# One core of Trainium2, attention and a gated MLP: the product and cast of a late pair's x^T moved to place 17, the first Strassen weights converted sooner

## The chip, the cores and the metric

The kernel runs on one core of a Trainium2 chip. The metric is the device time of one execution in microseconds (us); smaller is better. The engines are named as the profile names them: PE is TensorE (PEld its weight loads), DVE is VectorE, ACT is ScalarE, POOL is GpSimd and SP is SyncE, which issues most of the transfers. Each engine works off its own queue in order and meets the others through semaphores.

## What is computed

The reference, cut to its core (q and k are drawn about 5.7 times larger than its own setup draws them, the gate's weights 8 times; the three weight matrices arrive as float64):

```python
def _attn_ref(q, k, v):                      # q, k, v: 8 batches, 8 heads, 576 rows, 64 columns
    scores = (1.0 / np.sqrt(D)) * np.matmul(q, k.transpose(0, 1, 3, 2))
    scores = np.where(block_i >= block_j, scores, -1e9)      # blocks of 64 rows, causal
    scores = scores - np.max(scores, axis=-1, keepdims=True)
    attn = np.exp(scores)
    attn = attn / (np.sum(attn, axis=-1, keepdims=True) + 1e-09)
    return np.matmul(attn, v)

def _moe_ref(x, w_gate, w_val, w_out):       # x: 4608 x 512, d_ff = 1536
    gate = 1.0 / (1.0 + np.exp(-(x @ w_gate)))
    return (gate * (x @ w_val) @ w_out)
```

x is the attention's output with the heads side by side: 4608 tokens of 512 columns.

## The kernel before

**Attention, pair by pair.** The 64 heads are worked off as 32 pairs (two heads of a batch side by side on 128 partitions), `p` from 0 to 31; four pairs make a batch. Pairs 0 to 7 run in an early form. The late pairs, from 8 on, are what the change is about. For one of them, `prep` transposes keys and queries on VectorE (L436, into `KQ`) and splits them into a high and a low part: KH and QH by ScalarE (L476, L477), KL and QL by VectorE (L480, L481); GpSimd scales the first queries (L478) and copies the last ones into blocks (L486). `attend` then makes the scores (L397, into three double banks of PSUM), their maxima on VectorE (L536, L627), the exponentials on ScalarE (L551, L633), the 32x32 transposes of the exponentials on VectorE (L729 and on, into `ZV`), and the products with the values on TensorE in two halves (`z_run`). `z_out` copies these products from PSUM to `xT` on ScalarE (L778). The reciprocals of the sums go through memory (L639) and come back broadcast to all rows as `rb` (L647).

**finish.** `finish` ends a pair: GpSimd multiplies `xT` by `rb` (one product L806, two small ones L811), ScalarE casts the result to the high part `XH` (L813), GpSimd makes the low part `XL` (L828), and a store of `xT` is queued (L820). For the last pair VectorE does the products. `XH` and `XL` are the MLP's input.

**The MLP in between.** As soon as a batch's four pairs are done, its MLP with the first third of d_ff starts (`mlp1`): 144 matmuls of 128x512 a batch, 96 for gate and value (L163) and 48 for the output (L170). They are strewn between the attention's matmuls, so that TensorE has work while the other engines make the exponentials. Their results go to two banks named `m`. A gate is read by ScalarE (L202), a value by VectorE (L210); the product is split by ScalarE (L216, `hH`) and GpSimd (L217, `hL`); an output bank is evicted by ScalarE (L955) and stored (L958).

**What sets the order.** The order of a late pair is written out as a table, `REST`: a step's name and its number of places, 36 in all; at every place about one matmul of the MLP is dealt out. The steps are: AV (second half of the products of the pair before, and `z_out`), s and t (scores), sl (scores of the two smallest blocks), tr3, trt, tr2 (transposes), ml (maxima and exponentials of the two smallest blocks), r (reciprocals), trl, half (first half of this pair's products), k and q (both halves of `prep` for the next pair), and FX (`finish` for the pair before). Pair 8 has a table of its own (`JOIN`). In the late pairs an engine's instructions are chained in the order in which they are emitted (`line`); the gates, splits and low parts of the MLP are chained too, but the eviction L955 isn't: the scheduler places it. `LOADS` says at which place SyncE issues which transfer: v0, v1 (values), rb (the broadcast), xs (the store of `xT`), k0 to q3 (keys and queries), rr (the reciprocals to memory).

`KEEP` sets how many matmuls of the running MLP are kept back when a batch ends, to cover the time until the next batch's input is there; its second number counts from pair 8 on. Ahead of the products, `fill` adds a few tiny matmuls, so many that the count of TensorE's instructions fits a window.

**Behind the last pair** stand the last two MLPs (288 matmuls, what was kept back, and the last batch's tail), and under them the conversion of the first weights for the other two thirds of d_ff, which run as Strassen products (from L1340 on). `fetch_gv` loads float64 weights, `sums_gv` turns them into float32 and makes the sums, `split_gv` splits them; `x_sums` and `x_split` do the same for the tokens. The two first conversions are `early[0]` and `early[1]`; `early[0]` is fetched at the start of the last pair.

Of the kernel before, what the change touches and what calls it, by code (L numbers as in the profile page):

```python
# [20 lines left out]
N2 = 512  # L21
NX = 256
AHEAD = 3
KEEP = (52, 48)
WINDOW, MOST, FRONT = (140, 152), 24, 53

CONV_DUE = ([(0, 5), (0, 10), (1, 10), (2, 10), *((p, 9) for p in range(3, 7))], [(6, 1), (7, 2), (7, 8), (8, 1)])
# [2 lines left out]
         ("tr3", 1), ("r", 0), ("ld", 0))  # L30
ALONE = (("S3", 1), ("TR2", 1), ("warm", 0), ("k", 1), ("S2", 1), ("q", 1), ("m3", 0), ("m2", 0), ("TRt", 1), ("t", 1), ("TRl", 1), ("sl", 1), ("AV", 2),
         ("tr3", 1), ("r", 0), ("FX", 0), ("ld", 0))
REST = (("AV", 0), ("s", 0), ("t", 9), ("sl", 3), ("tr3", 2), ("trt", 3), ("tr2", 0), ("ml", 0), ("r", 0), ("trl", 0),
        ("half", 6), ("k", 4), ("q", 3), ("FX", 6))
JOIN = (("s", 0), ("t", 9), ("AV", 8), ("sl", 3), ("tr3", 2), ("trt", 3), ("tr2", 0), ("ml", 0), ("trl", 0), ("half", 2),
        ("r", 2), ("k", 2), ("q", 5))
TURN = (("s3", 1), ("TR2", 1), ("k", 0), ("s2", 1), ("TRt", 1), ("q", 0), ("t", 1), ("TRl", 1), ("sl", 1), ("AV", 1),
        ("tr3", 1), ("r", 0), ("tr2", 1), ("trl", 1), ("trt", 3))
N_FIRST = 7
LOADS = {0: "v0", 5: "rb", 8: "xs", 10: "k0", 12: "k1", 14: "k2", 16: "k3", 18: "v1", 23: "rr", 25: "q0", 27: "q1", 29: "q2", 32: "q3"}  # L40
JOIN_LOADS = {0: "k0", 3: "k1", 6: "k2", 9: "k3", 11: "v0", 16: "v1", 21: "q0", 24: "q1", 27: "q2", 30: "q3", 33: "rr"}
NV = 21
TICKS = 12
# [9 lines left out]
def attn_glu_kernel(ctx: ExitStack, tc: tile.TileContext, q, k, v, w_gate, w_val, w_out, out):  # L53
# [26 lines left out]
    def behind(ins, other):  # L80

        tc.add_manual_dep(ins, other.name, mybir.DependencyInfo(mybir.DependencyClass.NoSync,
                                                                mybir.DependencyReason.DATA), reason="order")
# [143 lines left out]
    with ExitStack() as s2:  # L227
# [105 lines left out]
        def load_in_turn(p, what, now):  # L333

            kind, i = what[0], what[1]
            dmas = ()
            if what == "rr":
                now(what)
            elif what in ("rb", "xs"):
                if waiting[what]:  # L340
                    waiting[what].pop()()
            elif kind == "v" and p + 1 < len(pairs):
                dmas = values_load(p + 1, int(i))
            elif kind in "kq" and p + 2 < len(pairs):
                dmas = (rows_load(p + 2, kind, int(i), nc.sync),)
            for dma in dmas:
                tc.add_manual_dep(dma.ins, dealt[0].name, mybir.DependencyInfo(mybir.DependencyClass.Sync,
                                                                               mybir.DependencyReason.DATA), reason="pace")
                line("q", dma)
                if kind == "v":  # L350
                    loads["SP"] = dma.ins
# [3 lines left out]
        last, loads, q_copied, recent = {}, {}, [], []  # L355
# [722 lines left out]
        def fetch_gv(g, q, gv, j, held=False, half=None):  # L1078
            raw, T = cv_tiles() if half is None else half_tiles()
            c = slice(None) if half is None else slice(half * P // 2, (half + 1) * P // 2)  # L1080
            src = (w_gate, w_val)[gv].rearrange("(kh c p) (a fh q n) -> kh c a q p fh n", kh=2, c=KC, fh=2, q=2, n=P)
            rawv = raw.rearrange("p (kh fh n) w -> p kh fh (n w)", kh=2, fh=2)
            fetch([rawv[:, kh] for kh in range(2)], [src[kh, j, F1 // 4 + g, q][:, :, c] for kh in range(2)], held)
            return raw, T

        def sums_gv(raw, T, held=False, **kw):

            Tn = T.rearrange("p s n -> p (s n)")
            m = 4 * T.shape[-1]
            to_f32(raw, Tn[:, :m], Tn[:, m:], held, **kw)  # L1090
            nc.vector.tensor_sub(out=T[:, 4], in0=T[:, 0], in1=T[:, 1])
            nc.vector.tensor_add(out=T[:, 1], in0=T[:, 1], in1=T[:, 3])
            nc.vector.tensor_sub(out=T[:, 5], in0=T[:, 3], in1=T[:, 4])
            return nc.vector.tensor_sub(out=T[:, 6], in0=T[:, 2], in1=T[:, 5]).ins
# [28 lines left out]
        def x_load(k, j, c0):  # L1123

            t0, nk = blocks[k]
            XB = cv.tile([P, 4, NX], F32, name="XB", bufs=2)
            v = XB[:, 0:4].rearrange("p (kh th) n -> p kh th n", kh=2)
            src = xT_d.rearrange("b (kh c p) s -> c b p kh s", kh=2, c=KC)[j]
            for th in range(2):
                a = 0  # L1130
                while a < NX:
                    b, o = divmod(t0 + th * nk + c0 + a, S)
                    m = min(S - o, NX - a)
                    d = nc.sync.dma_start(out=v[:, :, th, a:a + m], in_=src[b][:, :, o:o + m])
                    if "SP" in last2:
                        behind(d.ins, last2["SP"])
                    mark2("SP", d)
                    a += m
            return XB

        def x_sums(XB, eng, other=None):
            t1 = eng.tensor_sub(out=XB[:, 1], in0=XB[:, 1], in1=XB[:, 0])  # L1142
            if other:
                behind(t1.ins, other)
            return t1.ins
# [95 lines left out]
        early, early_x = [], []  # L1241

        def early_work(p, tick):

            if p == NP and tick == 0:
                n_conv[1] += 1
                next(conv_o)
            when = p - (n - 1), tick
            if when in ((0, 0), (1, 0)):
                early.append(fetch_gv(0, 0, 0, len(early)))  # L1250
                early_x.append(x_load(0, len(early_x), 0))
        for p in range(n + 1):
            early_work(p, 0)
            pr = prep(p + 1) if p + 1 < n else iter(())
            now = attend(p) if p < n else None
            tick = 0
            steps = (ALONE if p < NP else FIRST if p < N_FIRST else TURN if p == N_FIRST else
                     JOIN if p == N_FIRST + 1 else REST)
            ticks = sum(places for _, places in steps)
            lined[0] = line if N_FIRST < p < n else no_line  # L1260
            for what, places in steps:
# [23 lines left out]
                if p <= N_FIRST and new and p:  # L1285
                    rate = (left - KEEP[0]) / (4 * TICKS)
                elif p > N_FIRST and (new or what == steps[0][0]):
                    i = p % NP
                    rate = max(0, left - KEEP[1]) / (ticks - tick + (NP - 1 - i) * PLACES) if i or new else 1.0
                for _ in range(places if now else 6 if what == "AV" else 0):  # L1290
                    pe_ticks.append(pe_last[0])
                    acc += rate
                    while acc >= 1:
# [4 lines left out]
                        if ins is not None:  # L1298
# [7 lines left out]
                            if len(pe_ticks) > ahead_by:  # L1306
                                behind(ins, pe_ticks[-1 - ahead_by])
                    if now and p > N_FIRST and tick in (JOIN_LOADS if p == N_FIRST + 1 else LOADS):
                        load_in_turn(p, (JOIN_LOADS if p == N_FIRST + 1 else LOADS)[tick], now if p + 1 < n else lambda x: None)
                    tick += 1  # L1310
# [4 lines left out]
                load(p + 2, "v")  # L1315
            prev = now

        sums_gv(*early[0], alone=last["DVE"])
        x_sums(early_x[0], nc.vector, last["DVE"])
        sums_gv(*early[1], alone=last["DVE"])  # L1320
        s_at.close()
# [136 lines left out]
        early = [fetch_gv(0, 0, 1, j) for j in range(KC)]  # L1458
# [128 lines left out]
```

## Time and profile before

| | us |
|---|---|
| three runs, median | 1255.37 (1252.44 to 1256.64) |
| profiled execution | 1257.75 |
| its span, first to last instruction | 1256.0 |
| early pairs and first late pair, 0 to 149.71 | 149.71 |
| late pairs 9 to 31, 149.71 to 624.56 | 474.85 |
| MLP behind the last pair, 624.56 to 709.68 | 85.12 |
| Strassen products, 709.68 to 1256.0 | 546.32 |

TensorE is busy for 93% of the span, VectorE for 70%, ScalarE for 46%, GpSimd for 27%. These shares mix stages of different kinds, so the sections below go by stretch. The boundaries are the starts of the scores of a pair on TensorE (149.71 is pair 9, 215.00 pair 12) and the end of the last product with the values.

### The profile page before, as it was taken

Reading aid. Unit: us, or ns where it says so; the run is one execution under the profiler, and the core shown is the slowest. Engines: PE = TensorE matmul, PEld = TensorE weight load, DVE = VectorE, ACT = ScalarE, POOL = GpSimd, SP = SyncE. Lnnn points to the kernel's source line nnn. Section 1 sums busy time; section 2 is a strip of 40 time slices with the busy share of each in tenths; the row PEclk is TensorE's granted clock in tenths of the full one; section 3 lists DMA queues with packets and bytes.
Section 4 is the critical chain, followed back from the end, with each engine's and each line's share of the span. In section 5 each row is a group of like instructions: output and inputs, shape, how many; then the busy total and the mean of one; then the engine's idle time right before and its main releaser. Section 6 shows DMA issues by size and latency. Waiting matters only on the chain.

```text
span 1256.0 us, 31932 instructions
## 1 busy us (share of the span) xinstructions
PE 1162.5 (93%) x12843; PEld 927.7 (74%) x12843; DVE 878.0 (70%) x1751; ACT 573.3 (46%) x1372; POOL 345.0 (27%) x424
## 2 busy tenths in 40 slices
PE   8898978788897988879998999999999999999998
PEld 5565767566675767657776888888888888888888
DVE  5876845466464765656498795988999976758564
ACT  5876644445453554545424344354444432333222
POOL 3344424232323242332301111111111235151402
PEclk9998989899898998989999999999999999999999
DMA  7756454465655656546354214275377956253532
GB/s 175 181 133 156 120 124 116 123 161 136 149 141 126 174 118 171 139 112 161 113 156 133 69 51 134 55 201 148 72 217 256 313 178 203 84 184 108 161 105 81
DMA packets 345844, 180.29 MB, mean 144 GB/s; under 512 B 199072, under 2 KB 315616, under 8 KB 345056
## 3 DMA queue, kind: packets, MB, share of 16 engines
q1 hardware_dynamic: 342960, 175.20, 51.2%
q8 instruction: 101, 1.65, 0.6%
q10 hardware_dynamic: 2352, 2.00, 0.5%
q0 software_dynamic: 384, 1.05, 0.2%
q14 instruction: 47, 0.39, 0.1%
HBM read 130.58 MB, written 47.62 MB: 142 GB/s over the span
## 4 chain that ended last, share of the span: by engine, by line
PE 67%; DVE 10%; DMA 8%; POOL 6%; ACT 5%; issue 3%; SPq 1%; DVEq 0%; POOLq 0%; ACTq 0%
PE b L1340 27%; PE bank L397 9%; PE m L1425 8%; PE b L1425 8%; PE m L163 7%; PE m L170 6%; DMA rqk<-in_k_dram 3%; POOL xT L806 2%; ACT P L551 2%; DVE ZV L729 2%; DVE KQ L436 2%; PE bank L163 1%; DMA VR<-in_v_dram 1%; DVE nm L536 1%; DMA XB<-xT_d 1%
## 5 line engine op out<-in xcount | busy, mean ns | idle before, releaser
L1340 PE MATMUL b<-XH,w 128*128 128x512 f32 (+1 forms) x1120 | 320.6, 368 | 0.8 <-ACT p L1358 0.4
L1340 PEld LDWEIGHTS b<-XH,w 128*128 128x128 f32 x1120 | 203.5, 188 | 37.2 <-ACT p L1358 0.8
L1340 PE MATMUL b<-XL,w 128*128 128x512 f32 (+1 forms) x560 | 205.6, 368 | 0.0
L551 ACT ACTIVATE P<-bank,nm 128x512 f32<-128x512 f32 (+3 forms) x256 | 131.8, 524 | 41.4 <-DVE nm L536 41.1
L170 PE MATMUL m<-wo,hH 128*128 128x512 f32 x256 | 99.1, 447 | 36.1 <-ACT raws L955 31.9
L536 DVE TENSOR_REDUCE nm<-bank 128x2 f32<-128x1024 f32 (+3 forms) x128 | 100.9, 812 | 27.4 <-ACT bank L584 25.9
L1340 PEld LDWEIGHTS b<-XL,w 128*128 128x128 f32 x560 | 105.6, 189 | 17.5
L1157 ACT CAST XH<-XB 128x1024 fp32r<-128x1024 f32 (+1 forms) x72 | 66.9, 943 | 87.0 <-DVE XB L1155 49.6
L1425 PE MATMUL m<-wo,hH 128*128 128x512 f32 x288 | 93.2, 389 | 0.0
L163 PE MATMUL m<-XH,wg 128*128 128x512 f32 x240 | 86.9, 416 | 6.9 <-ACT raws L955 6.9
L170 PEld LDWEIGHTS m<-wo,hH 128*128 128x128 f32 x256 | 53.9, 213 | 53.0 <-ACT raws L955 34.1
L1425 PE MATMUL b<-wo,hH 128*128 128x512 f32 x288 | 92.9, 389 | 0.0
L1142 POOL TENSOR_TENSOR XB<-XB 128x256 f32<-128x256 f32 x30 | 24.6, 819 | 246.0 <-DMA XB<-xT_d 169.8
L729 DVE STREAM_TRANSPOSE ZV<-P 128x512 f32<-128x512 f32 (+1 forms) x192 | 84.8, 484 | 6.5 <-ACT P L551 6.5
L163 PE MATMUL m<-XH,wv 128*128 128x512 f32 x240 | 88.5, 424 | 0.0
L1160 DVE TENSOR_TENSOR XL<-XB,XH 128x1024 fp32r<-128x1024 f32 (+1 forms) x72 | 78.6, 1095 | 10.9 <-ACT XH L1157 10.7
L478 POOL TENSOR_SCALAR KQ<-KQ 128x128 f32<-128x128 f32 x24 | 22.4, 934 | 204.0 <-DVE KQ L436 204.0
L588 DVE MEMSET bank<- 64x128 f32 x24 | 4.0, 165 | 106.1 <-PE bank L397 106.1
L397 PE MATMUL bank<-ZV 32*64 32x48 f32 (+5 forms) x3680 | 73.6, 258 | 0.2 <-ACT P L551 0.2
L217 POOL TENSOR_TENSOR hL<-h,hH 128x512 fp32r<-128x512 f32 x28 | 37.5, 1338 | 119.5 <-ACT hH L216 119.5
L397 PEld LDWEIGHTS bank<-ZV 32*64 32x64 f32 (+1 forms) x3680 | 59.5, 130 | 14.4 <-issue 5.2
L1425 PEld LDWEIGHTS b<-wo,hH 128*128 128x128 f32 x288 | 54.1, 188 | 11.2
(220 smaller groups left out, 2504.7 us busy)
## 6 DMA issues: line engine op xcount, KB each, us to landing
part_d<-ost SPq DMA_DIRECT2D x56, 256.0 KB
XB<-xT_d SPq DMA_DIRECT2D x48, 256.0 KB
prr<-part_d SPq DMA_DIRECT2D x46, 256.0 KB
VR<-in_v_dram SPq DMA_DIRECT2D x12, 704.0 KB
ZV<-in_v_dram SPq DMA_DIRECT2D x12, 704.0 KB
xT_d<-xT SPq DMA_DIRECT2D x28, 288.0 KB
rqk<-in_k_dram SPq DMA_DIRECT2D x108, 72.0 KB
rqk<-in_q_dram SPq DMA_DIRECT2D x108, 72.0 KB
```

The source lines that it names most:

```text
L163: mm = nc.tensor.matmul(ps, lhsT=lh, rhs=rh, start=(i == 0), stop=(i == n - 1))
L170: mm = nc.tensor.matmul(ps, lhsT=lh[:, f, t * P:(t + 1) * P], rhs=rh, start=(f == i == 0), stop=(f == F1 - 1 and i == 2))
L217: low = lower.tensor_sub(out=hL, in0=h2, in1=hH.bitcast(F32))
L397: pe_last[:] = [nc.tensor.matmul(*args, **kw).ins]
L436: line("DVE", nc.vector.transpose(out=KQ[:, i], in_=rqks[p % 2][:, i]), late)
L536: line("DVE", nc.vector.tensor_reduce(out=nm[:, c0:c0 + 2], in_=ps[:, :, c:c + P * (i + 1)], axis=AX.X, op=ALU.max, negate=True), rest)
L551: line("ACT", nc.scalar.activation(out=dst, in_=src, func=AF.Exp, bias=nm[:, c0 + h:c0 + h + 1], accum_out=sm[:, 5 * h + i:5 * h + i + 1]) ...
L729: line("DVE", nc.vector.transpose(out=dst[:, :, :4 * ZG].rearrange("p b (g x) -> p b g x", g=4)[:, :, :i + 1, :32], in_=Pi[:, h].rearrange ...
L1157: cut = nc.scalar.copy(out=XO[j][0][:, a:b, c], in_=x)
L1160: sub = nc.vector.tensor_sub(out=XO[j][1][:, a:b, c], in0=x, in1=XO[j][0][:, a:b, c].bitcast(F32))
L1340: mm = nc.tensor.matmul(ps, lhsT=lh, rhs=rh, start=(first and k == 0), stop=(k == n - 1), skip_group_check=not first)
L1425: mm = nc.tensor.matmul(po[t], lhsT=lh[:, f, t * P:(t + 1) * P], rhs=rh, start=(half == 0 and i == 0), stop=(half == 1 and i == 5))
```

## The change

`FX` stood last in `REST`, behind k and q, with 6 places of its own, so that it was emitted at place 30. Now it stands behind ml, at place 17, and takes no place; q gets the six places. The broadcast is issued at place 2 instead of 5, the store of `xT` at place 7 instead of 8. `KEEP` keeps 40 matmuls back instead of 48. And `sums_gv(*early[0])`, the first conversion of Strassen weights, is emitted at place 18 of the last pair and no more behind all pairs.

```diff
-KEEP = (52, 48)
+KEEP = (52, 40)
...
-REST = (("AV", 0), ("s", 0), ("t", 9), ("sl", 3), ("tr3", 2), ("trt", 3), ("tr2", 0), ("ml", 0), ("r", 0), ("trl", 0),
-        ("half", 6), ("k", 4), ("q", 3), ("FX", 6))
+REST = (("AV", 0), ("s", 0), ("t", 9), ("sl", 3), ("tr3", 2), ("trt", 3), ("tr2", 0), ("ml", 0), ("FX", 0), ("r", 0), ("trl", 0),
+        ("half", 6), ("k", 4), ("q", 9))
...
-LOADS = {0: "v0", 5: "rb", 8: "xs", 10: "k0", ...
+LOADS = {0: "v0", 2: "rb", 7: "xs", 10: "k0", ...
...
             when = p - (n - 1), tick
+            if when == (0, 18):
+                sums_gv(*early[0], alone=last["DVE"])
...
-        sums_gv(*early[0], alone=last["DVE"])
         x_sums(early_x[0], nc.vector, last["DVE"])
         sums_gv(*early[1], alone=last["DVE"])
```

ScalarE in pair 12, from the small exponentials on, before (`raws` and `ost` are the two kinds of buffers into which L955 evicts a bank):

```order
L551 ACTIVATE P_2863,sm_107<-bank_2826,nm 128x256 x2
L551 ACTIVATE P_2866,sm_107<-bank_2826,nm 128x128 x2
L476 CAST KH<-KQ 128x576
L477 ACTIVATE QH<-KQ 128x448
L813 CAST XH_481<-xT 128x512
L955 ACTIVATE raws<-m 128x512
L955 ACTIVATE ost<-m 128x512
L778 COPY xT<-bank_2877 128x2x4x32
```

ScalarE in the same pair now:

```order
L551 ACTIVATE P_2841,sm_107<-bank_2787,nm 128x384 x2
L955 ACTIVATE raws<-m 128x512
L955 ACTIVATE ost<-m 128x512
L551 ACTIVATE P_2873,sm_107<-bank_2831,nm 128x256 x2
L551 ACTIVATE P_2876,sm_107<-bank_2831,nm 128x128 x2
L813 CAST XH_481<-xT 128x512
L476 CAST KH<-KQ 128x576
L477 ACTIVATE QH<-KQ 128x448
L955 ACTIVATE raws<-m 128x512
L778 COPY xT<-bank_2892 128x2x4x32
```

The cast L813 has gone ahead of KH and QH, and two evictions L955 that stood behind it have gone ahead of the small exponentials; a third stands behind QH.

GpSimd in the same pair before:

```order
L478 TENSOR_SCALAR KQ<-KQ 128x128
L486 COPY QBH<-QH 64x4x16 x2
L486 COPY QBL<-QL 64x4x16 x2
L806 TENSOR_TENSOR xT<-xT,rb 128x4x4x32
L811 TENSOR_TENSOR xT<-xT,rb 64x64 x2
L828 TENSOR_TENSOR XL_482<-xT,XH_481 128x512
```

GpSimd in the same pair now:

```order
L806 TENSOR_TENSOR xT<-xT,rb 128x4x4x32
L811 TENSOR_TENSOR xT<-xT,rb 64x64 x2
L828 TENSOR_TENSOR XL_482<-xT,XH_481 128x512
L478 TENSOR_SCALAR KQ<-KQ 128x128
L486 COPY QBH<-QH 64x4x16 x2
L486 COPY QBL<-QL 64x4x16 x2
```

The products and the low part have changed places with the scaling and the copies of the next pair's queries.

VectorE at the end of the last pair before (`cT` and `raw` belong to the weights, `XB` to the tokens):

```order
L729 STREAM_TRANSPOSE ZV<-P_8871 128x4x32 x2
L210 SCALAR_TENSOR_TENSOR h_9087<-t,m 128x512
L806 TENSOR_TENSOR xT<-xT,rb 128x4x4x32
L811 TENSOR_TENSOR xT<-xT,rb 64x64 x2
L1032 TENSOR_SCALAR cT<-raw 128x512
L1035 TENSOR_SCALAR cT<-raw 128x512
L1142 TENSOR_TENSOR XB<-XB 128x256
```

VectorE at the same place now:

```order
L1032 TENSOR_SCALAR cT<-raw 128x512
L1035 TENSOR_SCALAR cT<-raw 128x512
L1039 SCALAR_TENSOR_TENSOR cT<-raw,cT 128x512
L1041 SCALAR_TENSOR_TENSOR cT<-cT 128x512
L1043 TENSOR_SCALAR raw<-cT 128x512
L1045 SCALAR_TENSOR_TENSOR raw<-raw 128x512
L1046 TENSOR_TENSOR cT<-cT,raw 128x512
L1091 TENSOR_TENSOR cT<-cT 128x128
L1092 TENSOR_TENSOR cT<-cT 128x128
L1093 TENSOR_TENSOR cT<-cT 128x128
L1094 TENSOR_TENSOR cT<-cT 128x128
L806 TENSOR_TENSOR xT<-xT,rb 128x4x4x32
```

The whole first conversion, eleven instructions, stands ahead of the last pair's product with `rb`; an L210 between the last two rows here stays where it was. In the late pairs the MLP's matmuls are dealt out as 43 in pairs 9 to 11 each and 36 in each pair behind them (before: 40, 42, 41, then 36).

## Rows read from the trace of the kernel before

**Rows 1.** What TensorE waited for from 149 to 625: total us, times, longest.

```profile
PE m L170 <- ACT raws L955: 31.9, 5, 7.2
PE bank L397 <- ACT xT L778: 30.3, 16, 3.1
PE m L163 <- ACT raws L955: 6.9, 1, 6.9
```

**Rows 2.** Busy us by stretch (length first); last TensorE's clock, DMA share, GB/s.

```profile
core 0: us, PE busy (x) PEld busy (x) DVE busy (x) ACT busy (x) POOL busy (x), PEclk, DMA share, GB/s
244.57:260.65 16.08, 16.08 (x387) 13.02 (x382) 11.42 (x26) 9.30 (x29) 2.31 (x6) 1.00 0.76 190
260.65:278.12 17.47, 16.31 (x385) 12.92 (x380) 12.50 (x28) 9.90 (x30) 6.12 (x7) 1.00 0.67 156
278.12:298.72 20.60, 17.92 (x388) 13.95 (x383) 12.01 (x27) 9.88 (x30) 7.46 (x15) 0.92 0.55 128
298.72:326.61 27.89, 19.18 (x389) 14.57 (x384) 12.11 (x27) 10.41 (x31) 9.75 (x15) 0.82 0.47 113
...
149.71:215.00 65.29, 56.30 (x1157) 44.62 (x1152) 36.12 (x81) 30.09 (x90) 16.67 (x28) 0.90 0.55 133
215.00:624.56 409.56, 349.48 (x7627) 274.10 (x7622) 238.54 (x537) 197.69 (x600) 130.35 (x201) 0.92 0.57 138
...
624.56:709.68 85.12, 79.39 (x341) 63.73 (x336) 68.76 (x135) 31.50 (x50) 7.89 (x6) 0.98 0.39 119
```

**Rows 3.** Timeline of TensorE: start, us, instruction, idle time before it and releaser.

```profile
236.73 0.79 PE L170 MATMUL m<-wo,hH 128*128 128x512 f32 x1 [7.16 <-ACT raws L955]
...
267.89 0.39 PE L163 MATMUL m<-XH,wg 128*128 128x512 f32 x1
268.12 0.40 PE L163 MATMUL m<-XH,wv 128*128 128x512 f32 x1
```

**Rows 4.** Timeline of ScalarE ahead of that wait, pair 12.

```profile
231.14 0.67 ACT L476 CAST KH<-KQ 128x576 fp32r<-128x576 f32 x1 [2.43 <-DVE KQ L436]
...
235.56 0.62 ACT L813 CAST XH<-xT 128x512 fp32r<-128x512 f32 x1 [3.18 <-POOL xT L806]
236.08 0.59 ACT L955 ACTIVATE raws<-m 128x512 f32<-128x512 f32 x1
```

**Rows 5.** Timeline of GpSimd at the same place.

```profile
231.93 1.06 POOL L478 TENSOR_SCALAR KQ<-KQ 128x128 f32<-128x128 f32 x1 [8.61 <-DVE KQ L436]
...
234.27 1.26 POOL L806 TENSOR_TENSOR xT<-xT,rb 128x512 f32<-128x512 f32 x1
235.49 0.70 POOL L811 TENSOR_TENSOR xT<-xT,rb 64x64 f32<-64x64 f32 x2
```

**Rows 6.** Timeline, all engines: the pair without a wait, 244.57 to 260.65.

```profile
247.82 2.14 SPq L647 DMA_DIRECT2D rb<-r_r  x2
...
254.66 0.21 ACT L551 ACTIVATION_READ_ACCUMULATOR P<-bank,nm 128x1 f32 x1
...
257.31 0.67 ACT L476 CAST KH<-KQ 128x576 fp32r<-128x576 f32 x1 [2.44 <-DVE KQ L436]
...
258.69 0.71 DVE L481 SCALAR_TENSOR_TENSOR QL<-KQ,QH 128x448 fp32r<-128x448 f32 x1
...
260.65 0.50 PE L397 MATMUL bank<-KH,QH 64*128 64x512 f32 x2
```

**Rows 7.** Timeline: last pair's broadcast, VectorE and TensorE behind it.

```profile
621.38 1.24 SPq L647 DMA_DIRECT2D rb<-r_r  x2
...
627.18 0.69 DVE L806 TENSOR_TENSOR xT<-xT,rb 128x512 f32<-128x512 f32 x1 [3.97 <-DMA rb<-r_r]
...
632.61 1.28 DVE L1039 SCALAR_TENSOR_TENSOR cT<-raw,cT 128x512 uint32<-128x512 uint32 x2
...
639.71 1.16 DVE L1098 CAST w<-cT 128x896 fp32r<-128x896 f32 x2
...
671.20 0.50 PE L170 MATMUL m<-wo,hH 128*128 128x512 f32 x1 [3.67 <-ACT hH L216]
```

**Rows 8.** The instructions of line 478: ns min/median/max.

```profile
L478 POOL TENSOR_SCALAR KQ<-KQ x24: 528/1064/1142, 112.1 to 600.7; 128x128 f32<-128x128 f32 x24
```

More of the change, by code (lines that the diff above doesn't have):

```diff
@@ L39 @@
 N_FIRST = 7
-LOADS = {0: "v0", 5: "rb", 8: "xs", 10: "k0", 12: "k1", 14: "k2", 16: "k3", 18: "v1", 23: "rr", 25: "q0", 27: "q1", 29: "q2", 32: "q3"}
+LOADS = {0: "v0", 2: "rb", 7: "xs", 10: "k0", 12: "k1", 14: "k2", 16: "k3", 18: "v1", 23: "rr", 25: "q0", 27: "q1", 29: "q2", 32: "q3"}
 JOIN_LOADS = {0: "k0", 3: "k1", 6: "k2", 9: "k3", 11: "v0", 16: "v1", 21: "q0", 24: "q1", 27: "q2", 30: "q3", 33: "rr"}
```

## Prediction

> **What bounds the kernel now.** I read the stages first (busy time by stretch), then what TensorE waited for, then the order on the engines it waited for. From 709.68 us on TensorE is never idle for long, and before 149.71 the change moves two matmuls and no more, so the question is the stretch of the late pairs and the short one behind it. The 23 late pairs from 149.71 to 624.56 take 65.29 + 409.56 us, and TensorE is busy for 56.30 + 349.48 of it at a granted clock of 0.90 and 0.92 [rows 2]. The reader should look at four pairs that follow each other, with the same work: 16.08, 17.47, 20.60 and 27.89 us [rows 2]. The first is busy for all of its 16.08 us at clock 1.00. The others have idle time, and the last two also a clock of 0.92 and 0.82, which is a mean of stretches at 2.4 and at 1.2 GHz. So 16.08 us is what TensorE needs for a pair, and four pairs lose 82.04 - 4 x 16.08 = 17.7 us.
>
> Where the idle time comes from is in the list of TensorE's waits for this stretch, which has three lines only: 31.9 us (5 times) and 6.9 us (once) for an eviction at L955, and 30.3 us (16 times) for L778, which copies a pair's products out of their banks; together 69.1 us [rows 1]. Both are ScalarE's. ScalarE is not short of time; it stands at one instruction: after KH at 231.14 it sits idle for 3.18 us until GpSimd's product L806 is done, casts x^T at 235.56 and only then evicts at 236.08 [rows 4]. TensorE's next matmul starts at 236.73 after 7.16 us without work [rows 3]. GpSimd's product is late because of its place, not of its length: it stands behind the scaling L478 of the next pair's queries, which starts at 231.93, and so starts at 234.27 itself [rows 5].
>
> **The change part by part.**
>
> *The product and the cast at place 17.* The product (L806, L811), cast (L813) and low part (L828) are emitted ahead of the next pair's KH and QH instead of behind them. The cast then no longer stands ahead of L778 and of the evictions; that takes away all three lines, 69.1 us of waits, if the cast is ready at its new place. It stands now behind the last small exponential, which ends at 254.87 in a pair that had no wait, and ahead of KH, which starts at 257.31 there [rows 6]: a hole of 2.44 us, into which 0.62 us of cast [rows 4] must fit. Its condition is the broadcast of the reciprocals (L647). In the late pairs the trace doesn't show when that lands, since the product always came much later. The nearest row is the last pair's, where VectorE waited for it: issued at 621.38, used at 627.18, 5.8 us [rows 7]. From the issue at 247.82 [rows 6] that makes 253.6. The product needs 1.26 + 0.70 us [rows 5]: 255.6. The cast ends at 256.2, and KH still starts at 257.31. Bounds: 3 us earlier changes nothing; every microsecond later than 1.1 us is ScalarE's, and after another 1.25 us (VectorE's QL, 0.71 us long, ends at 259.40 and the scores start at 260.65 [rows 6]) TensorE's too. I take nothing, and 0.25 us a pair for jitter of this chain, between 0 and 0.5.
>
> On GpSimd the product and the low part now run ahead of L478, in a time in which GpSimd only waited for VectorE's transposes of the next pair; L478 follows these transposes as before. The store of x^T is let go at place 7, one place sooner, and the broadcast at place 2 and not 5; both still follow the load of the values on SyncE's queue, so I cost this at nothing, with at most 3 places of 0.23 us as a gain.
>
> *The clock.* Of the 17.7 us that four pairs lose, 82.04 - (16.08 + 16.31 + 17.92 + 19.18) = 12.6 us are idle; the other 5.1 are half clock behind the long waits, where the last of the four is busy for 19.18 us with the work of 16.08 [rows 2]. If the waits go, this goes with them. So I don't add waits and clock but count pairs. Twenty pairs from 215.00 to 624.56 at 16.08 us are 321.6 us against 409.56: **-88.0**, and +5.0 for the jitter.
>
> *KEEP 40 for 48.* Eight matmuls more are dealt out ahead of the first joint, eight fewer are left for the end. By the built order pairs 9 to 11 carry 43 each, the later ones 36. A matmul takes 0.23 us (267.89 to 268.12 [rows 3]), so these three pairs need 16.08 + 7 x 0.23 = 17.7 us, 53.1 in all. One eviction there still stands behind KH and QH and not far from its next use: +1.5, between 0 and the 6.9 us that this place costs now. 54.6 against 65.29: **-10.7**. The two matmuls of pair 8 cost 0.5, and the end gets 8 x 0.23 = 1.8 back.
>
> *New order of evictions.* In one pair of each later batch two evictions now stand between the exponentials, and by the count of matmuls ahead of their next use they come up to 0.5 us late: five batches at 0.4, **+2.0**, between 0 and 0.5 each (an exponential is waiting for VectorE there, so it isn't pushed).
>
> *First Strassen weights.* The first of the two conversions moves ahead of VectorE's last product. Two of them, interleaved, run from 632.61 to 639.71, 3.55 us each without their first two instructions; I take 4.4. In the last pair VectorE idles for 3.97 us at just this place, waiting for the broadcast [rows 7]. So at most 0.4 us is added ahead of the last cast, and 4.4 us leave the stretch 624.56 to 709.68, in which VectorE is busy for 68.76 of 85.12 us [rows 2]. TensorE's wait there is 3.67 us at 671.20 [rows 7]. Between 0 and 5 us; I take **-2.0**, less than half, since the transfer of x^T that holds VectorE up there moves only in part.
>
> Sum: -88.0 + 5.0 - 10.7 + 0.5 - 1.8 + 2.0 - 2.0 = **-95.0 us**. The profiled execution took 1257.75 us: 1162.8. It stands 2.4 us above the median of the three runs, so at the median 1160.4; I say **1161**.
>
> **The rivals.**
>
> *A: the waits go, but something holds a part of it.* Without pauses each chain of a pair, from scores over maxima, exponentials, reciprocals, KH and QL to the next scores, has to fit into 16.08 us every time; so far every such pair came after a long pause in which VectorE and GpSimd had caught up. For it: the second pair of the four shows 16.31 us of busy time and has its one wait, but no other. Against it: 11.42 of VectorE's and 9.30 of ScalarE's 16.08 us are busy, and the DMA share is 0.76 [rows 2]. One microsecond in each of 23 pairs, with a little half clock: 1161 + 23 + 8 = about **1190**.
>
> One form of it has a row. L478 takes 528 to 1142 ns for the same tile, 1064 in the middle [rows 8], so GpSimd is held up there. The Trainium skill, SBUF — State Buffer, "Who interferes with whom", says that VectorE with two SBUF inputs and GpSimd exclude each other on a shared port for a whole instruction, whoever comes first. By that rule, which speaks against this change, the low part L828, now shortly ahead of KL on VectorE, could block KL for its length; the spread of L478 agrees with it. In rows alone, as a mechanism of this kernel: KL is held up by an instruction of L806's size, 1.26 us [rows 5]. The chain behind KH has 1.25 us to spare, so by itself it costs nothing; where the cast has used that up by being late, it costs 1.26 x 23 = 29 us: 1161 + 29 = 1190, the same as A.
>
> *B: only one of the two families of waits goes.* If the evictions stay late where they are (38.8 us and their half clock), 30.3 us and a few of clock go: about **1220**. For it: the eviction isn't in the hand-written order of ScalarE, the scheduler places it. Against it: the built order shows it ahead of its next use in all batches.
>
> *C: slower.* ScalarE now meets the cast ahead of KH. If the broadcast lands late, ScalarE stands, and KH, QH, QL and the next scores behind it, in every pair. To eat up 95 us it takes 95 / 23 = 4.1 us a pair beyond the 1.1 + 1.25 us of cover: a landing 5.8 + 6.5 = 12.3 us after the issue. At 14 us the kernel would be 23 x 1.7 = 39 us slower than now, about **1294**. For it: in the late pairs the load of the values goes ahead of the broadcast, which it doesn't in the last pair. Against it: the 5.8 us there.
>
> *D: it doesn't do what it says*, the waits find another name in each pair: **1255**. Against it: the pair of 16.08 us.
>
> **How the numbers follow.** Forecast (1146 to 1175) 0.72; A (1175 to 1200) 0.14, of which 0.03 for the form with KL; B 0.06; C 0.03; D 0.02; better than 1146 0.03. The lower end is the sum without jitter and late evictions and with the whole 5 us at the weights: 1160.4 - 5 - 2 - 1.5 - 3 = 1149, less 3 for what the row of 16.08 us may hold of waits; the upper one takes in rival A. The range of 1146 to 1195 leaves out some 0.16. A measurement of this kernel tells about 0.3% from no change; faster by more than that: forecast, A, B and the better case, 0.95; within 0.02; slower 0.03.
>
> **What would show it.** The list of TensorE's waits should have lost both L955 and L778 lines, or hold under 10 us; ScalarE's wait at L813 should fall from 3 us to under 1 us each; the late pairs should each be near 16 to 16.5 us with clock 1.00, and L813 should start ahead of KH. Wrong are the terms in this order: a wait of KH or of the scores behind L813 (rival A or C), L955 still under TensorE's waits (B), late pairs at clock 0.8 without waits (the clock is not what I take it for), or a stretch from the last late pair to the first Strassen matmul that is longer than 83 us.

## The result, and the profile after

The changed kernel takes 1161.97 us in the median (1161.57 to 1165.48) against 1256.01 us before: a ratio of 0.9261, 95% interval 0.9234 to 0.9288. The forecast was 1161. The profiled execution took 1165.48 us, its span is 1163.7, so the profiles differ by 92.3 us where the sum had 95.0.

Busy time by stretch of the kernel after, columns as in [rows 2]: pair 9, two later pairs, pairs 12 to 31, and the stretch from the last product with the values to the first Strassen matmul.

```profile
148.67:169.61 20.94, 19.51 (x394) 15.53 (x389) 11.53 (x26) 10.47 (x31) 5.47 (x10) 0.92 0.64 159
...
221.69:237.79 16.10, 16.10 (x386) 13.01 (x382) 12.42 (x27) 9.81 (x30) 5.20 (x9) 1.00 0.80 197
...
336.41:353.71 17.30, 16.60 (x384) 12.92 (x380) 11.86 (x27) 10.55 (x31) 7.07 (x13) 1.00 0.75 184
...
205.01:535.45 330.44, 326.04 (x7628) 260.30 (x7623) 247.53 (x541) 198.21 (x597) 128.20 (x195) 1.00 0.71 171
535.45:617.16 81.71, 77.19 (x332) 62.48 (x329) 66.97 (x131) 31.79 (x51) 8.99 (x6) 0.98 0.40 122
```

Pairs 12 to 31 take 330.44 us, not 409.56, at a clock of 1.00, not 0.92. Every other pair takes 16.08 to 16.11 us, as the first of [rows 2]; the ones between take 16.4 to 17.6. What TensorE still waits for from pair 9 to the Strassen products answers to [rows 1]:

```profile
PE bank L397 <- ACT xT L778: 2.2, 5, 0.9
PE m L170 <- DVE h L210: 2.1, 1, 2.1
PE m L170 <- ACT hH L216: 2.0, 1, 2.0
PE m L170 <- ACT raws L955: 1.7, 5, 0.4
PE bank L397 <- issue: 1.7, 2, 1.4
```

The 69.1 us of [rows 1] have become 1.7 + 2.2 us. One later pair shows how (timeline of the kernel after, four engines, the pair from 353.71 to 369.82; it answers to [rows 4 to 6]):

```profile
356.98 2.03 SPq L647 DMA_DIRECT2D rb<-r_r  x2
...
363.20 1.28 POOL L806 TENSOR_TENSOR xT<-xT,rb 128x512 f32<-128x512 f32 x1 [10.31 <-DMA rb<-r_r]
...
363.79 0.21 ACT L551 ACTIVATION_READ_ACCUMULATOR P<-bank,nm 128x1 f32 x1
364.52 0.62 ACT L813 CAST XH<-xT 128x512 fp32r<-128x512 f32 x1 [0.52 <-POOL xT L806]
...
365.29 1.30 POOL L828 TENSOR_TENSOR XL<-xT,XH 128x512 fp32r<-128x512 f32 x1
...
366.75 0.68 ACT L476 CAST KH<-KQ 128x576 fp32r<-128x576 f32 x1 [1.61 <-DVE KQ L436]
...
367.46 0.76 DVE L480 TENSOR_TENSOR KL<-KQ,KH 128x576 fp32r<-128x576 f32 x1
```

The broadcast is used 6.2 us after its issue, the cast waits for 0.52 us, and ScalarE still stands idle for 1.61 us ahead of KH. So KH waits for VectorE, as in the pair of [rows 6], and not for the cast.

Every piece of that agrees with the prediction. The experiments say whether the pieces did what I said they did; one did not.

### The profile page after: what moved, and what is told of

Read it like the earlier page. It is cut to its first block, busy times and chain, and to the rows that moved or that the text cites. A ratio compares the mean times of both kernels' runs of the same rounds, so it can differ in the third digit from the quotient of the medians.

```text
span 1163.7 us, 31929 instructions
## 1 busy us (share of the span) xinstructions
PE 1133.7 (97%) x12835; PEld 911.2 (78%) x12835; DVE 885.2 (76%) x1751; ACT 575.4 (49%) x1372; POOL 347.7 (30%) x424
## 4 chain that ended last, share of the span: by engine, by line
PE 75%; DVE 11%; DMA 5%; ACT 4%; issue 3%; SPq 1%; POOL 1%; DVEq 0%; ACTq 0%; POOLq 0%
PE b L1341 27%; PE bank L397 14%; PE m L163 11%; PE b L1426 7%; PE m L1426 7%; PE m L170 5%; PE bank L163 2%; ACT P L551 2%; DMA rb<-r_r 1%; DVE nm L536 1%; DVE ZV L729 1%; DMA part_d<-ost 1%; DMA rqk<-in_q_dram 1%; DVE XL L1160 1%; PE bank L402 1%
## 5 line engine op out<-in xcount | busy, mean ns | idle before, releaser
L1426 PE MATMUL m<-wo,hH 128*128 128x512 f32 x288 | 93.2, 389 | 0.0
L170 PE MATMUL m<-wo,hH 128*128 128x512 f32 x256 | 84.7, 398 | 5.8 <-DVE h L210 2.1
L163 PE MATMUL m<-XH,wg 128*128 128x512 f32 x240 | 83.7, 407 | 0.0
L163 PE MATMUL m<-XH,wv 128*128 128x512 f32 x240 | 81.8, 398 | 0.0
L1426 PEld LDWEIGHTS m<-wo,hH 128*128 128x128 f32 x288 | 54.1, 188 | 11.2
L806 POOL TENSOR_TENSOR xT<-xT,rb 128x512 f32<-128x512 f32 x23 | 29.6, 1288 | 107.8 <-DMA rb<-r_r 69.2
L170 PEld LDWEIGHTS m<-wo,hH 128*128 128x128 f32 x256 | 47.0, 188 | 18.1 <-ACT raws L955 3.8
```

Source lines behind the costliest of these rows:

```text
L163: mm = nc.tensor.matmul(ps, lhsT=lh, rhs=rh, start=(i == 0), stop=(i == n - 1))
L170: mm = nc.tensor.matmul(ps, lhsT=lh[:, f, t * P:(t + 1) * P], rhs=rh, start=(f == i == 0), stop=(f == F1 - 1 and i == 2))
L806: line(engine, eng.tensor_mul(out=x4, in0=x4, in1=r4))
L1426: mm = nc.tensor.matmul(po[t], lhsT=lh[:, f, t * P:(t + 1) * P], rhs=rh, start=(half == 0 and i == 0), stop=(half == 1 and i == 5))
```

## The experiments

Times are medians; each ratio is against runs of the kernel before on the same chip.

**Experiment 1: the move alone.**

```diff
 (kernel before)
-REST = (... ("ml", 0), ("r", 0), ("trl", 0), ("half", 6), ("k", 4), ("q", 3), ("FX", 6))
+REST = (... ("ml", 0), ("FX", 0), ("r", 0), ("trl", 0), ("half", 6), ("k", 4), ("q", 9))
```

> The kernel before with the new place of FX alone: the broadcast stays at place 5, the store of x^T at 8, 48 matmuls are kept back, the weights are converted behind all pairs. Theory (the place of product and cast carries the gain): TensorE's waits at L955 and L778 go all the same; the broadcast lands some 1.3 us later, which the hole ahead of KH (1.6 us in the trace of after) just covers. About 1166 us: 1162 plus some 3 us for the weights, 0 to 3 us for the broadcast. Rival 1 (the broadcast has to be early as well): ScalarE's wait at L813 is over 1.5 us in most pairs, the scores start late, 1180 us or more. Rival 2 (the smaller KEEP carries the gain of pairs 9 to 11): these pairs take 60 us or more, 1172 us.

Measured: 1195.64 us, ratio 0.9521 (0.9499 to 0.9543). That is 30 us more than expected, and the reason is neither rival's: pairs 9 to 11 take 56.3 us, as after, and the broadcast is in time (ScalarE waits for L806 at the cast 16 times, at most 1.5 us). The L955 lines are still there (21.5 us in 5 waits, 3.1 in one, of the 38.8 before), while no wait at L778 is listed. The move has taken away one of the two families of waits and about a third of the other.

**Experiment 2: the changed kernel with KEEP 48.**

```diff
-KEEP = (52, 40)
+KEEP = (52, 48)
```

> The changed kernel with 48 matmuls kept back, not 40. Theory: KEEP only moves eight matmuls from pairs 9 to 11 to the end; TensorE has no pause in either, so pairs 9 to 11 get some 1.8 us shorter and the stretch behind the last pair 1.8 us longer, 1162 us within 2 us. Rival (what the prediction booked with KEEP is KEEP's): pairs 9 to 11 get longer by some us, up to 1171 us.

Measured: 1200.47 us, ratio 0.9563 (0.9541 to 0.9585): 38 us slower than with 40, against an expectation of "within 2 us". Eight matmuls kept back for the end cannot cost that by themselves. What TensorE waits for here, from pair 9 to the last product:

```profile
PE m L170 <- ACT raws L955: 20.1, 5, 4.4
PE m L163 <- ACT raws L955: 4.2, 1, 4.2
PE bank L397 <- POOL QBH L486: 0.9, 3, 0.4
```

One such wait, in pair 12 (timeline of this kernel, TensorE and ScalarE):

```profile
215.09 0.72 PE L170 MATMUL m<-wo,hH 128*128 128x512 f32 x2
...
216.57 0.40 PE L170 MATMUL m<-wo,hH 128*128 128x512 f32 x1
221.13 0.80 PE L170 MATMUL m<-wo,hH 128*128 128x512 f32 x1 [4.16 <-ACT raws L955]
...
217.13 0.62 ACT L813 CAST XH<-xT 128x512 fp32r<-128x512 f32 x1 [0.98 <-POOL xT L806]
219.35 0.67 ACT L476 CAST KH<-KQ 128x576 fp32r<-128x576 f32 x1 [1.60 <-DVE KQ L436]
220.02 0.58 ACT L477 ACTIVATE QH<-KQ 128x448 fp32r<-128x448 f32 x1
220.50 0.58 ACT L955 ACTIVATE raws<-m 128x512 f32<-128x512 f32 x1
```

The cast is out of the way, and the eviction is late all the same: ScalarE idles for 1.60 us until KH can start, does KH and QH, and only then evicts. The bank's twelfth matmul falls just behind the first half of the products (the run that starts at 215.09), so its eviction is queued behind KH and QH, and six matmuls later TensorE wants the bank. In the changed kernel the same two banks fill one run earlier and are evicted between exponentials (its ScalarE, pair 12):

```profile
211.78 0.19 ACT L551 ACTIVATION_READ_ACCUMULATOR P<-bank,nm 128x1 f32 x1
211.87 0.58 ACT L955 ACTIVATE raws<-m 128x512 f32<-128x512 f32 x1
212.35 0.59 ACT L955 ACTIVATE ost<-m 128x512 f32<-128x512 f32 x1
213.58 0.47 ACT L551 ACTIVATE P<-bank,nm 128x256 f32<-128x256 f32 x1 [0.65 <-DVE nm L536]
```

So a new theory: the place of the product makes the L778 waits; KEEP, through the phase of the output banks against KH and QH, makes the L955 waits. The next four runs test it.

**Experiment 3: KEEP 40 alone, in the kernel before.**

```diff
 (kernel before)
-KEEP = (52, 48)
+KEEP = (52, 40)
```

> The kernel before with KEEP 40 for 48 and nothing else. Theory (two families with two causes: the place of the product makes the waits at L778, the phase of the output banks those at L955): the L955 lines fall from 38.8 us to under 5 us, the L778 line grows from 30.3 us to some 45 us, because every pair now comes straight up to it; about 1246 us, 9 us faster than before. Rival (KEEP alone takes away its 38 us here as it does with the product moved): under 1225 us. Other rival (without the move it does nothing): 1255 us and both lines as before.

Measured: 1239.42 us, ratio 0.9888 (0.9860 to 0.9916); TensorE's waits from pair 9 to the last product:

```profile
PE bank L397 <- ACT xT L778: 45.4, 21, 3.4
PE m L170 <- ACT raws L955: 1.8, 5, 0.4
PE m L163 <- ACT ost L955: 1.6, 1, 1.6
```

The time is 7 us below the expected 1246; the waits are as the new theory says: L955 falls from 38.8 to 3.4 us, L778 grows from 30.3 to 45.4, because the pairs that used to lose time at an eviction now run straight into the other wait. That is why KEEP 40 is worth 16 us without the move and 38 with it.

**Experiment 4: KEEP 24**, two whole banks (24 matmuls) fewer than 48, and so the same phase.

```diff
-KEEP = (52, 40)
+KEEP = (52, 24)
```

> The changed kernel with 24 matmuls kept back, just two banks (24 matmuls) fewer than 48. Theory (phase of the output banks): by the built order one bank in each later batch fills with the first matmul behind the products' first half and is wanted six matmuls on, its eviction behind KH and QH, as with 48: five or six waits of 3 to 5 us at L955, 1190 to 1205 us. Rival (the fewer kept back, the better, or no effect): 1165 us or less. Other rival (too little left to cover the joint): waits at L163 for XH or XL.

Measured: 1195.81 us, ratio 0.9518 (0.9480 to 0.9556). The waits are back, this time where the next matmul in the bank is one of L163 (from pair 9 to the last product, as in the next two lists):

```profile
PE m L163 <- ACT raws L955: 21.1, 5, 4.4
```

Fewer kept back isn't better; 48 and 24 are slow alike, and 40 lies between them.

**Experiment 5: KEEP 36.**

```diff
-KEEP = (52, 40)
+KEEP = (52, 36)
```

> The changed kernel with 36 matmuls kept back. Theory (what counts is where the twelfth matmul of an output bank falls): by the built order the banks of each later batch fill ahead of the small scores and late in the second run of matmuls, none with its next use in the same run; no wait at L955 over 0.5 us: 1160 to 1164 us. Rival (the fewer kept back, the better): under 1155 us.

Measured: 1166.85 us, ratio 0.9290 (0.9256 to 0.9325). No L170 matmul waits for L955 any more, as expected; one of L163 still does, for 1.2 us, over the 0.5 us I had allowed. The time is some us over the expectation: another phase has its own wait, the last matmuls of L170 for a value's product on VectorE.

```profile
PE m L170 <- DVE h L210: 9.5, 5, 3.6
```

**Experiment 6: KEEP 48 with the eviction ahead of KH.** Evictions emitted behind a pair's second transposes join ScalarE's written order; the list `cold` says when.

```diff
-KEEP = (52, 40)
+KEEP = (52, 48)
...
-            nc.scalar.mul(out=ost, in_=ps, mul=0.5)
+            ev = nc.scalar.mul(out=ost, in_=ps, mul=0.5)
+            if cold[0]:
+                lined[0]("ACT", ev)
```

> The changed kernel with 48 matmuls kept back, and with an eviction L955 that is emitted behind a pair's second transposes put into ScalarE's written order. By the built order one eviction per batch moves, from behind KH and QH to between the cast L813 and KH. Theory (with 48 the output bank is full just behind the products' first half, where KH and QH stand ahead of its eviction, and KEEP costs nothing else): the five waits of some 4 us at L955 shrink to what is left behind the cast. With 48, TensorE wanted the bank at 216.97 us and the cast ended at 217.75, so 218.3 for the eviction: 1.3 us in each of five batches, and some half clock: 1168 to 1175 us. Rival (48 kept back costs by itself, at the joints of batches): 1195 us or more, as without the chaining.

Measured: 1173.92 us, ratio 0.9343 (0.9308 to 0.9379), in the expected range. With the same 48 kept back and one eviction a batch in another place, 26.6 of the 38.5 us come back. Most of KEEP's cost is the place of the eviction. Of the other 11.9 us two pieces can be read: TensorE still waits at L955, 7.2 + 2.0 us in the lines below and 1.2 us once at L163, against 24.3 us in experiment 2, and the stretch behind the last product takes 86.0 us, some 4 us more than in the kernel after, while pairs 9 to 11 are 3.3 us shorter (53.0 against 56.3). So some of the 11.9 us may be the 48 themselves; that is not shown.

```profile
PE m L170 <- ACT raws L955: 7.2, 5, 2.2
PE m L170 <- ACT ost L955: 2.0, 4, 0.5
```

**Experiment 7: the product alone moved**, the cast left at place 30 behind KH and QH.

```diff
-        ("ml", 0), ("FX", 0), ("r", 0), ... ("k", 4), ("q", 9))
+        ("ml", 0), ("FX1", 0), ("r", 0), ... ("k", 4), ("q", 3), ("FX2", 6))
```

FX1 emits L806 and L811, FX2 the cast, the store and the low part.

> The changed kernel with the products L806 and L811 at place 17, but cast, store and low part at place 30 behind KH and QH as before. Theory (it was GpSimd's product behind L478 that ScalarE stood for, and the cast's own place is worth little): ScalarE's wait at the cast is gone, the cast itself, 0.62 us, stands ahead of L778 again, so that the scores' bank is free 0.6 us later: half a us in each of 23 pairs, about 1173 us, with nothing over 1.5 us under TensorE's waits. Rival (the place of the cast on ScalarE is what counts): most of the 69 us of waits are back, over 1200 us.

Measured: 1167.11 us, ratio 0.9312 (0.9289 to 0.9335). ScalarE's list of waits has one line at the cast left, 2.4 us in the last pair, where VectorE makes the product, and TensorE waits at L778 for 4.2 us in all, not for 30.3 [rows 1] (nor for 45.7, as with KEEP 40 and nothing moved, experiment 12):

```profile
PE bank L397 <- ACT xT L778: 4.2, 7, 0.9
```

Nearly the whole gain of the move is GpSimd's order; the cast's own place is worth some 5 us by the medians and 2.3 by the profiled spans. I had expected 11, half a us in each pair; every other pair still takes 16.06 to 16.11 us, so the 0.6 us don't show in those.

**Experiment 8: the cast alone moved**, the products left behind L478 (diff shortened).

```diff
-                line("ACT", nc.scalar.copy(out=KS[0], ...   # KH
-                line("ACT", nc.scalar.mul(out=QS[0], ...    # QH
                 line("POOL", nc.gpsimd.tensor_scalar_mul(...  # L478
+                prev("fx")                                  # products, cast, low part
+                line("ACT", nc.scalar.copy(out=KS[0], ...
+                line("ACT", nc.scalar.mul(out=QS[0], ...
```

> The changed kernel with the cast ahead of KH and QH on ScalarE, but the products behind L478 on GpSimd, as before the change; the cast so waits for transposes, L478 and product. Theory: KH starts some 3.7 us later than now, 1.25 us of it covered: 2.4 us in each of 23 pairs, 55 us: 1217 us, and up to 1257 us with half clock behind each wait; TensorE's waits name KH, QL or KL, no L955. Rival (the cast's place on ScalarE alone takes the waits away): under 1180 us.

Measured: 1251.92 us, ratio 0.9987 (0.9964 to 1.0009): nothing is left of the gain, although KEEP is 40 here. This is rival C as a mechanism: ScalarE stands at the cast for 94.9 us (19 times) with KH behind it, and the scores wait for what follows KH (lines here are 4 further down):

```profile
PE bank L397 <- DVE QL L485: 22.9, 21, 1.9
PE bank L397 <- ACT QH L482: 20.1, 19, 2.5
PE bank L397 <- ACT xT L782: 8.2, 10, 0.9
```

**Experiments 9 and 10: the broadcast later.** At place 5 and at place 11, in place of 2:

```diff
-LOADS = {0: "v0", 2: "rb", 7: "xs", ...
+LOADS = {0: "v0", 7: "xs", ..., 5: "rb"}      (11: "rb")
```

> The changed kernel with the broadcast issued at place 5, not 2. In the trace of after the cast ends 1.6 to 1.9 us ahead of KH, and a place is 16.1 / 36 = 0.45 us. Theory (the cover counts): product and cast come 1.3 us later, still ahead of KH; ScalarE's waits at L813 grow by about 1.3 us a pair, TensorE's don't: 1162 us within 2 us. Rival (the early broadcast is needed): scores wait in each pair, 1170 us or more.

Measured: 1163.58 us, ratio 0.9283 (0.9265 to 0.9300): no different from the kernel after. But the edit moves nothing. SyncE's transfers stand in the same order as in the kernel after, the broadcast right behind the load of the values, and it is issued at the same time (timeline of this kernel, the pair shown above, whose first scores start at 351.54):

```profile
354.82 1.85 SPq L647 DMA_DIRECT2D rb<-r_r  x2
```

That is 354.82 - 351.54 = 3.28 us after the pair's first scores; in the kernel after it is 356.98 - 353.71 = 3.27, and before the change, at place 5, 247.82 - 244.57 = 3.25 [rows 6]. So this run doesn't test the cover. It shows that "place 2 instead of 5" was no change either.

> The changed kernel with the broadcast at place 11. Theory (the cover counts): 9 places of 0.45 us are 4.0 us, 2.4 of them beyond the hole of 1.6 us; KH is late by 2.4, the scores by 2.4 - 1.25 = 1.2 us in each of 22 pairs: 26 us, and up to as much for half clock: 1188 to 1210 us. Rival (ScalarE's late cast delays nothing that TensorE waits for): 1162 to 1168 us. Other rival (the waits of the kernel before come back): L955 and L778 are the names under TensorE's waits, not KH and QL.

Measured: 1175.14 us, ratio 0.9377 (0.9360 to 0.9394), 13 us more than after, about half of the least I had expected. ScalarE waits 50.4 us (20 times) at the cast, not 10.0 (15 times), and TensorE's L778 line is 6.7 us. My step from places to time was wrong. Here the broadcast stands behind the first load of keys on SyncE's queue (the same pair, first scores at 357.64):

```profile
364.02 1.25 SPq L647 DMA_DIRECT2D rb<-r_r  x2
```

It is issued 364.02 - 357.64 = 6.38 us after the pair's first scores, 3.11 us later than in the kernel after, and used 369.16 - 364.02 = 5.14 us after its issue, not 6.22. So the product starts 369.16 - 357.64 = 11.52 us after the first scores, in the pair shown above 363.20 - 353.71 = 9.49: 2.0 us later, not 4.0. KH so starts 371.01 - 357.64 = 13.37 us after the first scores and not 366.75 - 353.71 = 13.04: 0.33 us late, well inside the slack of 1.25 us ahead of the next scores. But that slack is eaten into by something else (timeline of this kernel, the same pair):

```profile
370.48 0.62 ACT L813 CAST XH<-xT 128x512 fp32r<-128x512 f32 x1 [2.56 <-POOL xT L806]
371.01 0.67 ACT L476 CAST KH<-KQ 128x576 fp32r<-128x576 f32 x1
...
371.24 1.28 POOL L828 TENSOR_TENSOR XL<-xT,XH 128x512 fp32r<-128x512 f32 x1
...
371.71 1.43 DVE L480 TENSOR_TENSOR KL<-KQ,KH 128x576 fp32r<-128x576 f32 x1 [0.73 <-ACT KH L476]
```

KL takes 1.43 us here and 0.76 in the kernel after. I come back to that at the end. The two delays together, 0.33 + 0.67 us, still fit into the slack, and this pair takes 16.20 us all the same. What is lost lies mostly in the pairs between: pairs 14, 16 and so on to 28 take 17.4 to 17.9 us here and 16.4 to 17.3 in the kernel after, with a wait at L778 in each of them. How the late KH and KL lead to those waits is not shown.

**Experiment 11: the weights converted at the end again.**

```diff
-            if when == (0, 18):
-                sums_gv(*early[0], alone=last["DVE"])
...
+        sums_gv(*early[0], alone=last["DVE"])
         x_sums(early_x[0], nc.vector, last["DVE"])
```

> The changed kernel with the first conversion of weights behind all pairs again. Theory: only the stretch from the last product with the values to the first Strassen matmul changes, from 81.7 to 84 to 85 us, since VectorE is what it waits for; 1164 to 1165 us. Rival (that stretch got shorter by KEEP alone, the weights were hidden): it stays within 0.7 us of 81.7, 1162 us.

Measured: 1165.76 us, ratio 0.9291 (0.9273 to 0.9310); its interval overlaps that of the kernel after, so the time doesn't decide. The stretch from the last product to the first Strassen matmul takes 82.10 us, against 81.71: by the stretch the rival was right, it got shorter by KEEP alone. (In experiment 3, with KEEP 40 and the old place of the weights, it is 81.55; with KEEP 48 it is 85.12 before and 86.21 in experiment 2. In experiment 12, which has KEEP 40, the old place of the product and the earlier weights, it is 84.7: there the earlier conversion makes it some 3 us longer than in experiment 3.)

**Experiment 12: all but the move.** The changed kernel with FX back at place 30.

```diff
-        ("ml", 0), ("FX", 0), ("r", 0), ... ("q", 9))
+        ("ml", 0), ("r", 0), ... ("q", 3), ("FX", 6))
```

> The changed kernel with FX back at place 30: broadcast at place 2, KEEP 40 and the earlier weights alone. Theory: the three lines of waits of the kernel before stay (some 60 to 70 us), the time is 1250 to 1257 us, of which up to 4 us less are the weights. Rival (the parts beside the move bring a good part): under 1240 us.

Measured: 1242.68 us, ratio 0.9907 (0.9880 to 0.9935). The L778 line is 45.7 us in 21 waits, L955 3.5 us: experiment 3 once more. Half of the expectation fell, that all three lines stay, and the time lies between the expected 1250 and the rival's 1240. Beside KEEP, the earlier weights and the broadcast at place 2 add no gain that shows.

None of these is faster than the changed kernel.

## Why the prediction was right, point by point

**The sum, by stretch.** Measured on the two profiles, against the terms on record:

| stretch | predicted | measured |
|---|---|---|
| pairs 12 to 31 | -88.0 + 5.0 + 2.0 = -81.0 | 330.44 - 409.56 = -79.1 |
| pairs 9 to 11 | -10.7 | 56.34 - 65.29 = -9.0 |
| ahead of pair 9 | +0.5 | 148.67 - 149.71 = -1.0 |
| behind the last pair | -1.8 - 2.0 = -3.8 | 81.71 - 85.12 = -3.4 |
| Strassen products | 0 | +0.2 |
| sum | -95.0 | -92.3 |

**Right: the pair of 16.08 us as the measure.** Counting pairs, not adding up waits and clock, made the clock a part of the count, and TensorE did come up to that pair every second time. The 7.0 us for jitter and late evictions were 330.44 - 321.6 = 8.8; of these TensorE's list names 1.7 us at L955, where the sum had 2.0, and 2.2 at L778. The rest was not traced to a cause.

**Right: the cover of the cast.** Predicted was a cast that ends 1.1 us ahead of KH, with the broadcast used 5.8 us after its issue; the pair shown has 6.2 us, and the cast ends at 365.14, 1.6 us ahead of KH. Two of its terms were off, in opposite directions: the broadcast came 0.4 us later, and the 0.70 us of L811 were not needed, since the cast starts at 364.52, as soon as L806 has ended, and doesn't wait for L811 (it does so only in the last three pairs). The rows on record showed that already: L813 at 235.56 [rows 4] behind the end of L806, 234.27 + 1.26, while L811 had begun at 235.49 [rows 5]. Experiment 9 left the broadcast where it was; experiment 10 used up the whole cover. The earlier place of the broadcast, costed as a gain of nothing to 3 places, gained nothing: its issue didn't move.

**Wrong: "that takes away all three lines, 69.1 us of waits".** This step gave the whole to the new place of product and cast. It takes away L778 and about a third of L955. With KEEP 48 the move leaves 24.6 us (experiment 1) and 24.3 us (experiment 2) of the 38.8 us at L955: what ScalarE stood at has gone, but KH and QH still stand ahead of the eviction. The rest, 38 of the 94 us, is KEEP's (experiment 2), which I had booked as eight matmuls that change places. The total was right all the same, not by this argument but because the check against rival B was made on the built order of the whole change, KEEP included: "the built order shows it ahead of its next use in all batches". That was true, of both edits together. Had the change left KEEP at 48, the argument as I wrote it would have given about the same 1161 us, the kernel takes 1200, and rival B with its 1220 would have been the nearer.

**Wrong in size: the parts at the end.** The weights were put at -2.0 and show 0.4 us in the stretch; KEEP was put at -1.8 there and shows some 3.5 (85.12 to 81.55 in experiment 3). The errors cancel. Where the other 1.7 us of KEEP come from I did not follow up.

**Missed in size: pair 9.** In pairs 9 to 11 I put 1.5 us on an eviction behind KH and QH. It cost nothing. What does cost is a stop in the middle of the products of pair 9, for which the profile names no releaser, and matmuls at half clock behind it (timeline of TensorE, kernel after):

```profile
157.15 1.06 PE L397 MATMUL bank<-ZV 32*64 32x48 f32 x76
159.64 0.96 PE L397 MATMUL bank<-ZV 32*64 32x48 f32 x68 [1.43 <-issue]
...
161.87 0.63 PE L163 MATMUL m<-XH,wg 128*128 128x512 f32 x1
...
166.13 0.39 PE L163 MATMUL m<-XL,wv 128*128 128x512 f32 x1
```

Pair 9 takes 20.94 us at clock 0.92, and pairs 10 and 11, with the same 43 matmuls, 17.70 each. In experiments 3, 7 to 9, 11 and 12, all with KEEP 40, the stop comes at the same product, with 0.9 to 1.5 us; with KEEP 48, 36 or 24 there is none over 0.3 us in that pair. In experiment 10, with KEEP 40 too, there is none either. Its cause stays open.

**The rivals.** A's general form did not come: the 7.0 us that the forecast held for it were 8.8, not 31 more. Its form with KL did not come about in the kernel after, where KL has a median of 758 ns, but it is real: experiments 8 and 10 have it. C needs the cast to come late by more than the cover, and in experiment 8 it does. D did not come: the lines that stand in place of the 69.1 us add up to 9.7.

## What to carry to other kernels

Where an in-order engine stands at one instruction, look for the order of the engine that feeds it: here it was GpSimd's order that held up ScalarE, and moving GpSimd's product alone brings all but some 5 us of what the whole move brings. Two waits on the same engine can have two causes: before one edit gets both, ask what stands ahead of each waiting instruction once the edit is made, with the other edits left out. A number that shifts a stream of work against another (KEEP) acts through its phase: judge it by where each buffer fills and is wanted again, not by how much work it moves.

## What the runs showed of the hardware

**VectorE's KL is held up by GpSimd's L828.** All instructions of L480 (KL), ns min/median/max, in the kernel after and in experiment 10:

```profile
L480 DVE TENSOR_TENSOR KL<-KQ,KH x24: 743/758/1500, 113.7 to 517.8; 128x576 fp32r<-128x576 f32 x24
```

```profile
L480 DVE TENSOR_TENSOR KL<-KQ,KH x24: 757/1428/1498, 111.9 to 528.9; 128x576 fp32r<-128x576 f32 x24
```

In experiment 10 each KL that starts while GpSimd's L828 runs takes 0.95 to 1.50 us, and ends some 0.6 us after that has ended; each later one without such an overlap takes 0.76. In the kernel after one KL only meets L828, the one at 499.81: it is the 1500 ns of its row. The Trainium skill, SBUF — State Buffer, "Who interferes with whom", says that a VectorE instruction with two SBUF inputs contends with a GpSimd instruction that reads SBUF, and that who holds the shared ports keeps them for the whole instruction; the trace agrees, nearly: 0.6 us behind L828's end is a little less than the 0.76 us that KL takes alone. I had priced it at the full 1.26 us. As KL starts 0.47 us into L828 it costs about 0.67, and the kernel after avoids it because L828 ends ahead of KH.

**Places aren't time.** For a transfer a place sets its order on SyncE's queue. At places 2 and 5 the broadcast stood behind the same load of values and was issued 3.27 and 3.28 us after the pair's first scores; at place 11 it stood behind a load of keys and was issued 6.38 us after them. Nine of 36 places made the product 2.0 us later, where a share of the pair's 16.1 us would have made 4.0. A step's time is read from the rows of the stretch in which it stands.
